# Feature maps with one ScalarE operation, an in-place min on GpSimd and the VectorE join; third layer's tokens scaled on ScalarE

## The chip, the core and the metric

The kernel runs on one core of a Trainium2 chip. A core has five engines that run their own instruction streams in order: TensorE (PE, matrix products into PSUM), VectorE (DVE), ScalarE (ACT), GpSimd (POOL) and SyncE (SP, which here issues DMAs). They wait for each other through semaphores. The metric is the device time of one execution in microseconds (us), the median of several runs.

## The reference

`x` is 2048 tokens of 1024 values (one batch). Four layers are applied, each as `x = x + f(layernorm(x))`: layer 0 and layer 2 are a linear attention with the same weights, layer 1 and layer 3 a gated feed-forward block (3584 wide) with the same weights. Of the attention, this is what matters here:

```python
q, k, v = split(x @ wqkv)                              # 32 heads of 32
phi = lambda t: where(t > 0, t + 1, exp(t)) + 1e-6     # the feature map
pq, pk = phi(q), phi(k)
kv = einsum("bhsd,bhse->bhde", pk, v)
z  = einsum("bhsd->bhd", pk)
o  = einsum(pq, kv) / (einsum(pq, z) + 1e-6)
return o @ wo
```

The feature map can be written without a branch as `max(t, 0) + min(exp(t), 1) + 1e-6`, which equals `max(t, 1e-6) + exp(-max(-t, 0) + 1e-6)` up to terms of 1e-6.

## The kernel before

Tokens lie in 16 tiles of 128 (t), four of which make a quarter (q, or `sc`). The whole `x` is resident in SBUF. An attention layer (`layer_A`, l = 0 or 2) goes through these stages:

- **Layer norm** (`ln_norm`): mean and variance on VectorE, the root on ScalarE, then the scaling of a tile of 128x1024. In layer 0 and, but for its first four tiles, in layer 2 the scaling is one VectorE `tensor_scalar` (`ln_scale`, L183); the first four tiles of layer 2 use a small VectorE operation for the shift (L214) and a ScalarE `Identity` activation (L216). A DMA then transposes the tile into `xnT`.
- **Projections** of q and k. Layer 0 makes *units* (`project`, L506): eight matmuls of 128x512 into one PSUM bank, for one tile of tokens and half the columns of q or k. Units take banks from a pool of four ("a") and, every third one, from a pool of two ("b"); the last row of units (keys of the last quarter) uses the four alone. Layer 2 makes some units too, but takes the q of quarters 0 and 1 and the k of quarters 2 and 3 by a seven-product scheme (`blocks`), described below.
- **Feature map** (`phi`, L444 to L458), once for each unit or block result, 128 in all, 16 of them in units whose quarter 3 q is made later (`q3`). ScalarE writes `relu(-ps)` to an SBUF tile `e` (L448), then `exp(-e + 1e-6)` in place (L449); VectorE joins them as `max(ps, 1e-6) + e` into the bf16 home of q or k (L452, called the *join*). The join is the last reader of the PSUM bank.
- **Key sum** (`k_sum`): for each half tile of k, GpSimd adds the joined keys into `ksum` (L527; the first of each half is a copy, L525). It waits for the join.
- **Products** `k^T x` (`m_products`), folded into `wo` later.

**The seven-product scheme** (`blocks`, L656 to L727). Each of four token groups j makes four results of 128x512 from the PSUM banks X, Y, Z and an SBUF tile V, in four steps: `one` (product 1 into X, copy Y from X, product 5, copy to V), `two` (product 2 into X, feature map of X; product 6 into Y; Z = Y + V on VectorE, L712), `three` (product 7 into Y; V = Y + V on VectorE, L716; feature map of V; product 3 into Z, feature map of Z) and `four` (product 4 into Y, feature map of Y). X and Z come from pool "a", Y from pool "b". For the k blocks, called the **K blocks** from here on, groups 0 and 1 run interleaved, then groups 2 and 3 (L933), and the copies Y from X and V of groups 1 to 3 are VectorE copies (L681). In the trace the tiles are `qx`, `qy`, `qz` and `qm` (V), for q and for k alike; the k results land in `slab`.

**What sets the order.** The program is written unit by unit with a list of delayed jobs (`later`). A scheduler then fixes the instruction order on each engine, except in stretches marked `manual_schedule`, where the engines named keep the written order. On the chip each engine runs its list strictly in order, so an instruction that waits holds back all behind it.

Of the kernel before, what the change touches and what calls it, by code (L numbers as in the profile page):

```python
# [92 lines left out]
class _Net:  # L93
    def __init__(self, tc, ctx, x_d, wqkv_d, wo_d, wg_d, wu_d, wd_d, out_d):
# [39 lines left out]
        self.inner = {}  # L134
        self.later = _Later()
        self.phi_lag = 0

        from concourse.masks import make_identity
        self.ident = self.const.tile([P, P], BF16, name="ident")
# [47 lines left out]
    def ln_norm(self, layer, t):  # L187

        nc = self.nc
        if layer % 2:  # L190
            return self.ln_norm_sums(layer, t)
        src = self.xb[t] if layer == 0 else self.x[t]
        if layer == 2 and t < self.NS:
            mv = self.acc[:, 2 * t:2 * t + 2]
        else:
            stats = self.small.tile([P, 2, nc.vector.BN_STATS_DIM], F32, tag="stats")
            for c in range(2):
                self.ln_stat(t, src, c, stats)
            if layer == 2:
                mv = self.small.tile([P, nc.vector.BN_AGGR_DIM], F32, tag="mv")  # L200
                nc.vector.bn_aggr(out=mv, in_=stats)
            else:
                mv, rstd = self.ln_rstd(stats)

        def scale(rstd=None if layer == 2 else rstd):
            if rstd is None:
                with self.tc.issue_after(self.last_exp.ins):
                    rstd = self.ln_root(mv)
                return lambda: scale(rstd)
            if layer % 2 == 0 and (layer, t // QT) != (2, 0):  # L210
                return self.ln_scale(src, mv, rstd, self.xn_home(layer, t))
            xn = self.temp([P, self.D], F16, name="xnb") if layer % 2 else self.xn_home(layer, t)
            shift = self.small.tile([P, 1], F32, tag="shift")
            nc.vector.tensor_scalar(out=shift, in0=mv[:, 0:1], scalar1=rstd[:, 0:1], scalar2=-1.0,  # L214
                                    op0=ALU.mult, op1=ALU.mult)
            nc.scalar.activation(out=xn, in_=src, func=ACT.Identity, scale=rstd[:, 0:1],  # L216
                                 bias=shift[:, 0:1])
            return xn

        return scale  # L220
# [220 lines left out]
        for j in range(QT):  # L441
            self.ln_at(first + j * step, layer, q * QT + j, lag, after)

    def phi(self, ps, out):  # L444

        nc = self.nc
        e = self.temp()
        nc.scalar.activation(out=e, in_=ps, func=ACT.Relu, scale=-1.0)  # L448
        self.last_exp = nc.scalar.activation(out=e, in_=e, func=ACT.Exp, scale=-1.0, bias=self.eps6[:, 0:1])  # L449

        def join():
            self.last_phi = nc.vector.scalar_tensor_tensor(out=out, in0=ps, scalar=1e-6, in1=e,  # L452
                                                           op0=ALU.max, op1=ALU.add)

        if self.phi_lag:
            self.later.at(self.phi_lag, join)
        else:
            join()  # L458
# [21 lines left out]
    def layer_A(self, l, last_ln):  # L480
# [392 lines left out]
        def run(*lists):  # L873

            n = max(len(u) for u in lists)
            for i in range(n):
                for u in lists:
                    if i < len(u):
                        u[i]()
                        later.tick()  # L880
# [26 lines left out]
        def quarter0():  # L907
            self.phi_lag = 3 if l == 0 else 0
            run(first)
            self.phi_lag = 0  # L910

        if l == 0:
            with self.tc.manual_schedule(engines={mybir.EngineType.DVE, mybir.EngineType.SP,
                                                  mybir.EngineType.Activation}):
# [23 lines left out]
            run(row_major(k_unit, q), row_major(q_unit, q))  # L938
        if l == 0:
            run(row_major(k_unit, self.NQ - 1))  # L940
        with self.tc.manual_schedule(engines={mybir.EngineType.DVE, mybir.EngineType.Pool}):
            q3 = row_major(q_unit, self.NQ - 1)
            out0 = column_major(out_unit, 0)
# [868 lines left out]
```

## Time and profile before

| what | value |
|---|---|
| median of 3 runs | 1438.27 us (1438.09 to 1438.8) |
| the profiled execution | 1439.99 us, of which the span from the first to the last instruction is 1437.9 us |
| PE busy | 1427.1 us (99%) |
| DVE busy | 1045.2 us (73%) |
| ACT busy | 623.3 us (43%) |
| POOL busy | 309.3 us (22%) |
| projections of layer 0 | some 6 to 106 us of the span |
| projections of layer 2 | some 732 to 823 us, the K blocks from some 797 us |

An engine is busy in a stretch while one of its instructions executes. A row of the grouped views gives line, engine, operation, tiles (out<-in), shapes, count, then busy time and mean ns of one, then the engine's idle time just before the group and what ended it. A row of one line's view gives the shortest, median and longest duration. A row of the timeline gives start and duration in us and, in brackets, the idle time of the engine before it with what ended it.

### The profile page before, as it was taken

To read this page: it belongs to the slowest core of one execution; us is meant where nothing else is said; L and a number is where in the kernel's file an instruction comes from. 1 tells how busy PE (TensorE), PEld (TensorE's weight loads), DVE (VectorE), ACT (ScalarE), POOL (GpSimd) and SP (SyncE) were. 2 spreads that over 40 slices of the span, in tenths; PEclk is the share of its full clock that TensorE was granted. 3 is DMA by queue.
4 is the path that set the end of the run, shared out by engine and by line. 5 is a ranking of instruction groups with operands and counts; after the bars stand their busy time and mean duration, and the time that the engine had idled before them with its cause. 6 is when DMAs were issued, how large, how long until landed. Compare 5 with 4: busy or idle time off the path is not lost.

```text
span 1437.9 us, 21394 instructions
## 1 busy us (share of the span) xinstructions
PE 1427.1 (99%) x7720; PEld 739.7 (51%) x7748; DVE 1045.2 (73%) x2013; ACT 623.3 (43%) x1143; POOL 309.3 (22%) x220
## 2 busy tenths in 40 slices
PE   9999999999999999999999999999999999999998
PEld 4444444444455444545654444445554565555557
DVE  7978698778685666558778886866766864766895
ACT  7872564333325244332058725733443433444301
POOL 1453860010100011110032477510111011111102
PEclk9999999999999999999999999999999999999999
DMA  9950787898559999966983218998878699975575
GB/s 286 240 162 8 172 209 202 278 335 288 200 192 294 323 367 345 291 216 199 302 277 93 70 22 234 287 274 262 268 225 294 228 304 335 274 229 174 193 260 183
DMA packets 367865, 337.74 MB, mean 235 GB/s; under 512 B 110032, under 2 KB 327760, under 8 KB 366736
## 3 DMA queue, kind: packets, MB, share of 16 engines
q1 hardware_dynamic: 359184, 313.57, 73.1%
q10 hardware_dynamic: 7136, 18.88, 3.4%
q0 software_dynamic: 1440, 3.93, 0.7%
q8 instruction: 60, 0.98, 0.3%
q14 instruction: 45, 0.37, 0.1%
HBM read 246.87 MB, written 64.82 MB: 217 GB/s over the span
## 4 chain that ended last, share of the span: by engine, by line
PE 91%; DVE 3%; DMA 2%; ACT 2%; SPq 1%; issue 1%; ACTq 0%; DVEq 0%
PE ps L506 11%; PE yu L1301 9%; PE yg L1301 9%; PE xg L1301 6%; PE xu L1301 6%; PE dy L1447 6%; PE dx L1447 5%; PE i L1154 5%; PE ps L789 4%; PE zu L1301 3%; PE zg L1301 3%; PE my L588 3%; PE dyT L1489 2%; PE mv L588 2%; PE mx L588 2%; PE dy L1489 2%
## 5 line engine op out<-in xcount | busy, mean ns | idle before, releaser
L1301 PEld LDWEIGHTS <-w 128*128 128x128 f16 (+1 forms) x2768 | 270.4, 98 | 297.2 <-issue 4.6
L506 PE MATMUL ps<-w,xnT 128*128 128x512 bf16 x768 | 169.9, 380 | 0.6 <-ACT xnT L361 0.2
L1381 POOL TENSOR_TENSOR h<-m5u,m5g 128x512 f16<-128x512 f32 x28 | 37.1, 1326 | 425.3 <-DVE m5u L1377 252.5
L506 PEld LDWEIGHTS <-xnT 128*128 128x128 bf16 x768 | 74.4, 98 | 90.3 <-issue 1.8
L1301 PE MATMUL xg<-xnT,w 128*128 128x512 f16 x448 | 115.5, 379 | 0.0
L1301 PE MATMUL xu<-xnT,w 128*128 128x512 f16 x448 | 115.0, 380 | 0.0
L1489 PEld LDWEIGHTS <-h 128*128 128x128 f16 x1008 | 98.6, 98 | 12.9
L1381 POOL TENSOR_TENSOR h<-c22u,c22g 128x512 f16<-128x512 f32 x28 | 36.0, 1285 | 289.8 <-DVE c22u L1377 247.8
L1447 PEld LDWEIGHTS <-h 128*128 128x128 f16 x616 | 60.3, 98 | 71.8 <-issue 0.3
L1301 PE MATMUL yu<-s,w 128*128 128x512 f16 x376 | 96.5, 379 | 0.5 <-DVE zu L1357 0.5
L1301 PE MATMUL yg<-s,w 128*128 128x512 f16 x376 | 96.9, 379 | 0.0
L449 ACT ACTIVATE e<-e,eps 128x512 f32<-128x512 f32 x128 | 91.0, 720 | 3.2
L736 POOL TENSOR_TENSOR kvc<-pq,kvc 128x1024 f32<-128x1024 bf16 x32 | 78.5, 2452 | 53.1 <-DVE den L741 32.8
L789 PE MATMUL ps<-T,pqT 128*128 128x512 bf16 x374 | 83.0, 380 | 0.5
L1328 DVE TENSOR_TENSOR h<-yu,r 128x512 f16<-128x512 f32 x56 | 38.6, 690 | 53.8 <-PE yu L1301 53.8
L1325 ACT ACTIVATE r<-yg 128x512 f32<-128x512 f32 x56 | 33.4, 597 | 101.3 <-PE yg L1301 101.3
L527 POOL TENSOR_TENSOR kvc<-kvc,slab 128x512 f32<-128x512 f32 x46 | 57.2, 1249 | 75.9 <-DVE slab L452 72.7
L1447 PE MATMUL dx<-w,h 128*128 128x512 bf16 x327 | 72.5, 380 | 0.5
L448 ACT ACTIVATE e<-ps 128x512 f32<-128x512 f32 x92 | 54.2, 590 | 28.4 <-PE ps L506 27.9
L1154 PEld LDWEIGHTS <-x 128*128 128x128 f16 x504 | 49.3, 98 | 33.5 <-issue 1.9
L1325 ACT ACTIVATE r<-zg 128x512 f32<-128x512 f32 x56 | 32.9, 587 | 76.7 <-PE zg L1301 76.7
L748 POOL TENSOR_TENSOR pq<-pq,den 128x1024 bf16<-128x1024 bf16 x32 | 61.1, 1909 | 6.8 <-DVE den L743 6.8
(286 smaller groups left out, 2630.6 us busy)
## 6 DMA issues: line engine op xcount, KB each, us to landing
w<-in_B_W_gate_dram SPq DMA_DIRECT2D x56, 512.0 KB, 6.4
w<-in_B_W_up_dram SPq DMA_DIRECT2D x56, 512.0 KB, 6.0
w<-ddT SPq DMA_DIRECT2D x21, 896.0 KB, 6.4
w<-td SPq DMA_DIRECT2D x18, 896.0 KB, 5.0
w<-dd SPq DMA_DIRECT2D x18, 896.0 KB, 5.9
x<-away SPq DMA_DIRECT2D x30, 512.0 KB, 7.5
away<-x SPq DMA_DIRECT2D x24, 512.0 KB, 8.1
w<-in_B_W_down_dram SPq DMA_DIRECT2D x12, 896.0 KB, 6.1
```

Of the source, the lines that this page charges most:

```text
L449: self.last_exp = nc.scalar.activation(out=e, in_=e, func=ACT.Exp, scale=-1.0, bias=self.eps6[:, 0:1])
L506: nc.tensor.matmul(by_row(ps), lhsT=self.xnT[l, l_q][:, kt, j * P:(j + 1) * P], rhs=w[:, kt, :].rearrange("p (b i d) -> p i b d", i=R, d=H ...
L588: nc.tensor.matmul(banks[j], lhsT=A(i)[:, j * P:(j + 1) * P], rhs=B(i), start=start and i == 0, stop=i == NS - 1, skip_group_check=True)
L736: nc.gpsimd.tensor_tensor(out=prod, in0=pq_of[sc, j], in1=zrow, op=ALU.mult)
L748: nc.gpsimd.tensor_tensor(out=heads(pq), in0=heads(pq), in1=den[:, :].unsqueeze(2).to_broadcast([P, D // HD, HD]), op=ALU.mult)
L789: nc.tensor.matmul(ps, lhsT=pqT[sc][:, g, j * P:(j + 1) * P], rhs=T[g // 4][:, g % 4, n2 * NW:(n2 + 1) * NW], start=(g == 0), stop=(g == G ...
L1154: nc.tensor.matmul(b[:, w, :], lhsT=B[p][:, w, k, :], rhs=A[p][:, k, :], start=start and w == 0 and k == 0, stop=k == 1, skip_group_check= ...
L1301: nc.tensor.matmul(ps, lhsT=W[w][m][:, k, :], rhs=A[m][:, k, :], start=start and k == 0, stop=k == 3, skip_group_check=True)
L1325: self.last_relu = nc.scalar.activation(out=out, in_=ps, func=ACT.Relu)
L1381: nc.gpsimd.tensor_tensor(out=h[:, 3, :], in0=V["u"], in1=V["g"], op=ALU.mult)
L1447: nc.tensor.matmul(banks[j], lhsT=A(k)[:, j * P:(j + 1) * P], rhs=w[:, i, :], start=start and k == 0, stop=k == self.U - 1, skip_group_che ...
L1489: nc.tensor.matmul(out, lhsT=A[i // 2][:, i % 2, j * P:(j + 1) * P], rhs=B[m][:, i, :], start=start and i == 0 and j == 0, stop=i == NK - ...
```

## The change

Two edits. In `phi`, under a flag that is set from the first quarter of an attention layer to the end of its q and k projections (112 of the 128 feature maps), ScalarE now does one operation, `e = exp(ps)` straight from PSUM (or from V); GpSimd does `e = min(e, 1) + 1e-6` in place; the VectorE join is `max(ps, 0) + e`. The 16 maps of `q3` stay as they were. In `ln_norm`, the `tensor_scalar` scaling remains for layer 0 only: the other twelve tiles of layer 2 now go the way of its first four (a 128x1 shift on VectorE, the scaling on ScalarE).

```diff
@@ in __init__
         self.phi_lag = 0
+        self.phi_pool = False
@@ in ln_norm
-            if layer % 2 == 0 and (layer, t // QT) != (2, 0):
+            if layer == 0:
                 return self.ln_scale(src, mv, rstd, self.xn_home(layer, t))
@@ phi
-    def phi(self, ps, out):
+    def phi(self, ps, out, low=1e-6):
         nc = self.nc
         e = self.temp()
-        nc.scalar.activation(out=e, in_=ps, func=ACT.Relu, scale=-1.0)
-        self.last_exp = nc.scalar.activation(out=e, in_=e, func=ACT.Exp, scale=-1.0, bias=self.eps6[:, 0:1])
+        if self.phi_pool:
+            low = 0.0
+            self.last_exp = nc.scalar.activation(out=e, in_=ps, func=ACT.Exp)
+            nc.gpsimd.tensor_scalar(out=e, in0=e, scalar1=1.0, scalar2=1e-6, op0=ALU.min, op1=ALU.add)
+        else:
+            nc.scalar.activation(out=e, in_=ps, func=ACT.Relu, scale=-1.0)
+            self.last_exp = nc.scalar.activation(out=e, in_=e, func=ACT.Exp, scale=-1.0,
+                                                 bias=self.eps6[:, 0:1])
         def join():
-            self.last_phi = nc.vector.scalar_tensor_tensor(out=out, in0=ps, scalar=1e-6, in1=e,
+            self.last_phi = nc.vector.scalar_tensor_tensor(out=out, in0=ps, scalar=low, in1=e,
                                                            op0=ALU.max, op1=ALU.add)
@@ in layer_A, ahead of the first quarter
+        self.phi_pool = True
         if l == 0:
...
             run(row_major(k_unit, self.NQ - 1))
+        self.phi_pool = False
         with self.tc.manual_schedule(engines={mybir.EngineType.DVE, mybir.EngineType.Pool}):
```

The scheduler also places the instructions anew. Three places matter for what follows.

GpSimd, K blocks of layer 2. `kvc` holds `ksum`; rows that end in `slab_1` add the columns 0 to 511 or 512 to 1023 of tiles 8 to 11 (results X and Z), rows that end in `slab_3` those of tiles 12 to 15 (V and Y). Before:

```order
L527 TENSOR_TENSOR kvc_6878<-kvc_6878,slab_1_7604 128x512 [waits DVE_49,Pool_49] x2
L527 TENSOR_TENSOR kvc_6878<-kvc_6878,slab_3_7636 128x512 [waits DVE_49]
L527 TENSOR_TENSOR kvc_6878<-kvc_6878,slab_1_7604 128x512 [waits DVE_49,Pool_49]
L527 TENSOR_TENSOR kvc_6878<-kvc_6878,slab_3_7636 128x512 [waits DVE_49,Pool_49]
L527 TENSOR_TENSOR kvc_6878<-kvc_6878,slab_1_7604 128x512 [waits DVE_49,Pool_49]
L527 TENSOR_TENSOR kvc_6878<-kvc_6878,slab_3_7636 128x512 [waits DVE_49]
```

After the change, from the min of X of group 0 (the last of the first row) to the sums of the first two groups:

```order
L452 TENSOR_SCALAR e<-e 128x512 [waits DVE_49,Activation_49]
L534 TENSOR_TENSOR kvc_6886<-kvc_6886,slab_1_7628 128x512 [waits DVE_49]
L452 TENSOR_SCALAR e<-e 128x512 [waits Activation_49]
L534 TENSOR_TENSOR kvc_6886<-kvc_6886,slab_1_7628 128x512 [waits DVE_49]
L452 TENSOR_SCALAR e<-e 128x512 [waits Activation_49] x2
L534 TENSOR_TENSOR kvc_6886<-kvc_6886,slab_3_7660 128x512 [waits DVE_49]
L452 TENSOR_SCALAR e<-e 128x512 [waits Activation_49]
L534 TENSOR_TENSOR kvc_6886<-kvc_6886,slab_1_7628 128x512 [waits DVE_49,Pool_49]
L452 TENSOR_SCALAR e<-e 128x512 [waits Activation_49]
L534 TENSOR_TENSOR kvc_6886<-kvc_6886,slab_3_7660 128x512 [waits DVE_49,Pool_49]
L452 TENSOR_SCALAR e<-e 128x512 [waits Activation_49] x2
```

The mins of the eight results of groups 0 and 1 now stand between the key sums on the same list, in the order X0, X1, V0 and Z0, V1, Z1, Y0 and Y1; the three rows that follow in the list (not shown) are the sums of Z1, Y0 and Y1, and only then come the mins of X2 and X3.

VectorE, K blocks, where group pair 0, 1 meets pair 2, 3. Before:

```order
L452 SCALAR_TENSOR_TENSOR slab_3_7636<-qm_7598,e 128x512 [waits DVE_49,Activation_49]
L681 COPY qy_7693<-qx_7688 128x512 [waits PE_49]
L452 SCALAR_TENSOR_TENSOR slab_1_7604<-qz_7628,e 128x512 [waits Activation_49]
L681 COPY qm_7700<-qv_7695 128x512 [waits DVE_49,PE_49]
L452 SCALAR_TENSOR_TENSOR slab_3_7636<-qy_7577,e 128x512 [waits Activation_49]
L452 SCALAR_TENSOR_TENSOR slab_3_7636<-qy_7591,e 128x512 [waits Activation_49]
L681 COPY qy_7707<-qx_7702 128x512 [waits DVE_49,PE_49]
L681 COPY qm_7714<-qv_7709 128x512 [waits PE_49]
```

After the change:

```order
L459 SCALAR_TENSOR_TENSOR slab_3_7660<-qm_7622,e 128x512 [waits DVE_49,Pool_49]
L459 SCALAR_TENSOR_TENSOR slab_1_7628<-qz_7652,e 128x512 [waits Pool_49]
L688 COPY qy_7717<-qx_7712 128x512 [waits PE_49]
L459 SCALAR_TENSOR_TENSOR slab_3_7660<-qy_7601,e 128x512 [waits Pool_49]
L459 SCALAR_TENSOR_TENSOR slab_3_7660<-qy_7615,e 128x512 [waits Pool_49]
L688 COPY qm_7724<-qv_7719 128x512 [waits DVE_49,PE_49]
L688 COPY qy_7731<-qx_7726 128x512 [waits DVE_49,PE_49]
L688 COPY qm_7738<-qv_7733 128x512 [waits PE_49]
```

The joins now wait for GpSimd instead of ScalarE, and the copies of Y2 and V2, which TensorE needs for groups 2 and 3, each stand behind more joins than before: the copy of Y2 behind the join of Z1, the copy of V2 behind the joins of Y0 and Y1.

GpSimd, layer 0, keys of the last two quarters (`slab_2` and `slab_3`). Before, the list held key sums alone there. After the change:

```order
L452 TENSOR_SCALAR e<-e 128x512 [waits Activation_49] x2
L534 TENSOR_TENSOR kvc_160<-kvc_160,slab_2_826 128x512 [waits DVE_49]
L452 TENSOR_SCALAR e<-e 128x512 [waits Activation_49] x2
L534 TENSOR_TENSOR kvc_160<-kvc_160,slab_3_1097 128x512 [waits DVE_49]
L452 TENSOR_SCALAR e<-e 128x512 [waits Activation_49]
L534 TENSOR_TENSOR kvc_160<-kvc_160,slab_3_1097 128x512 [waits DVE_49]
```

Two mins stand to one key sum while q and k units alternate, and one to one in the last row of k units.

## The prediction

> **What bounds the kernel now.** I read the busy line first, then the busy times by stretch, then the chain of waits inside the one stretch where TensorE is not full.
>
> ```profile
> PE 1427.1 (99%) x7720; PEld 739.7 (51%) x7748; DVE 1045.2 (73%) x2013; ACT 623.3 (43%) x1143; POOL 309.3 (22%) x220
> 20.00:125.00 105.00, 104.89 (x487) 47.57 (x487) 88.16 (x168) 77.72 (x141) 41.84 (x30) 1.00 0.65 185
> 732.00:835.00 103.00, 102.24 (x471) 46.09 (x472) 89.12 (x163) 80.17 (x146) 38.34 (x32) 1.00 0.37 109
> 800.00:823.00 23.00, 22.47 (x103) 10.01 (x103) 18.10 (x28) 16.87 (x29) 13.78 (x12) 1.00 0.29 92
> L506 PE MATMUL ps<-w,xnT 128*128 128x512 bf16 x391 | 84.6, 379 | 0.0
> ```
>
> The stretch rows read: length, then busy time of PE, weight load, DVE, ACT, POOL, then the clock. In the projections of layer 0 (20 to 125 us) TensorE idles 105.00 - 104.89 = 0.11 us, in those of layer 2 (732 to 835 us) 103.00 - 102.24 = 0.76 us, and 0.53 us of that lies in the K blocks. The change touches nothing that TensorE does, and the clock is 1.00 throughout, so **0.9 us is all that can be won**. What can be lost is open: every feature map holds a PSUM bank, and what is late there stops TensorE. The unit matmuls come every 84.6 / 391 = 0.216 us, so a unit of eight takes 1.73 us.
>
> The chain that ended last, in the K blocks (start, length, what):
>
> ```profile
> 804.47 0.69 DVE qm L716
> 805.19 1.11 ACT e L448 x2
> 806.30 1.22 ACT e L449 x2
> 807.52 1.00 ACT e L448 x2
> 808.52 0.62 ACT e L449
> 809.16 0.65 DVE slab L452
> 810.58 0.69 DVE qy L681
> 811.85 0.61 DVE qm L681
> 812.50 1.02 PE qv L690 x4
> ```
>
> From 804.5 to 812.5 us the chain leaves TensorE and runs through V of group 0, four ACT operations for V0 and Z0, three for V1 and Z1, the join of V1 and the copies of Y2 and V2. TensorE arrives with hardly any time to spare. In the units of layer 0 it never leaves TensorE.
>
> **The change part by part.** Prices of the operations:
>
> ```profile
> L448 ACT ACTIVATE e<-ps 128x512 f32<-128x512 f32 x92 | 54.2, 590 | 28.4 <-PE ps L506 27.9 <-DVE stats L166 0.4
> L449 ACT ACTIVATE e<-e,eps 128x512 f32<-128x512 f32 x128 | 91.0, 720 | 3.2
> L452 DVE SCALAR_TENSOR_TENSOR slab<-ps,e 128x512 bf16<-128x512 f32 x30 | 20.5, 683 | 8.5 <-ACT e L449 8.3
> L452 DVE SCALAR_TENSOR_TENSOR slab<-qm,e 128x512 bf16<-128x512 f32 x4 | 4.4, 1089 | 2.6 <-ACT e L449 2.6
> L527 POOL TENSOR_TENSOR kvc<-kvc,slab x46: 1151/1158/1532, 18.0 to 827.5; 128x512 f32<-128x512 f32 x46
> L525 POOL CAST kvc<-slab x2: 609/611/613, 14.7 to 17.5; 128x512 f32<-128x512 bf16 x2
> L183 DVE TENSOR_SCALAR slab<-x,mv,rstd 128x1024 bf16<-128x1024 f32 x8 | 8.5, 1056 | 1.2 <-ACT rstd L177 1.1
> L216 ACT ACTIVATE x<-x,shift,rstd 128x1024 bf16<-128x1024 f32 x3 | 3.7, 1232 | 0.0
> ```
>
> *ScalarE.* 112 maps lose one operation. The exp now reads PSUM, as the old relu did at 0.59 us, against 0.59 + 0.72 = 1.31 us for both: 112 x 0.72 = 81 us off an engine at 43%. The scaling of twelve layer-2 tiles adds 12 x 1.23 = 14.8 us to it and takes about 12 x 1.06 = 12.7 us from VectorE. Outside the K blocks neither engine sets TensorE's pace, so both are worth 0 by themselves, at best the 0.2 us of layer-2 idle time outside the K blocks. In the chain above the relus go: V1's exp would end some 1.9 us earlier (three relus of about 0.6).
>
> *GpSimd.* 112 in-place min-and-add operations on 128x512 f32. The trace has no such operation. The nearest rows: one input, same size, the CAST at 0.61 us; two inputs, same size, the key sum at 1.16. One input is the nearer kin, but it reads four bytes here and does two operations; I take **0.65 us**, bounds 0.61 and 1.16.
>
> The Trainium skill ("GPSIMD Engine Reference", section Performance versus the Vector engine) gives 769 ns for the best case of a loop over 512 elements. By that the K blocks below would cost about 1.2 us more; no run here shows the operation, and the CAST of 0.61 is already under that figure.
>
> *K blocks of layer 2.* GpSimd's list there has, by the order after the change, up to the min of Z1: six mins and the key sums of X0, X1, V0, Z0, that is 6 x 0.65 + 4 x 1.16 = 8.5 us of work. X0 is ready for the first min when its exp ends:
>
> ```profile
> 800.67 0.60 ACT L448 ACTIVATE e<-qx 128x512 f32<-128x512 f32 x1 [1.97 <-PE qx L690]
> 811.32 1.02 PE L690 MATMUL qx<-w,xnT 128*128 128x512 bf16 x4 [0.32 <-DVE qy L681]
> 814.30 1.02 PE L690 MATMUL qx<-w,xnT 128*128 128x512 bf16 x4
> 813.57 0.68 DVE L681 COPY qy<-qx 128x512 f32<-128x512 f32 x1
> ```
>
> so at 801.3. Without idle time GpSimd would finish at 809.8. But the sum of X0 waits for its join (about 1.0 us of idle, a VectorE addition and a join of 0.68), and the joins of V0 and V1 take two SBUF operands: the row of `qm` shows 1.09 us against 0.68, so they and GpSimd hold each other up, some 0.6 us each. That makes 809.8 + 1.0 + 1.2 = 812.0 for the min of Z1, then its join (0.68) and the copy of Y2 (0.69), which now stand in this order: 813.4. TensorE's second product of group 2 started at 811.32 behind that copy: **+2.1 us**. Then GpSimd sums V1 and does the mins of Y0 and Y1 (1.16 + 1.30, and 0.3 of waiting): 814.5, join of Y1, and the copies of V2 and Y3, which end near 816.5. TensorE took the copy of Y3 (813.57 + 0.68) at 814.30: +2.2, plus about 0.7 because its product 5 of group 3, behind the copy of V2, no longer overlaps. In the second pair the mins of X2 and X3 stand behind three key sums (3.5 us), and X2's join stands ahead of the addition for Z3, about +1.1 us more. Sum for the K blocks: 2.2 + 0.7 + 1.1 = **+4.0 us**. Ten mins lie on this path, so each 0.1 us of the min's price is worth 1 us: 3.6 at 0.61, 9 at 1.16. If the waits of 2.2 us are all hidden, it is 0.5 or less. What comes after has cover: the second key product (mx) of `m_products` starts 32 matmuls, 6.9 us, after the last K product.
>
> *Layer 0.* Here the cover is PSUM: six banks in rotation, so a join may end 5 x 1.73 = 8.6 us after its unit; 5.2 us in the last row.
>
> ```profile
> 76.60 0.60 ACT L448 ACTIVATE e<-ps 128x512 f32<-128x512 f32 x1 [0.21 <-PE ps L506]
> 81.23 0.68 DVE L452 SCALAR_TENSOR_TENSOR pq<-ps,e 128x512 bf16<-128x512 f32 x1
> 40.00:60.00 20.00, 20.00 (x95) 9.03 (x94) 20.00 (x35) 14.88 (x30) 9.52 (x8) 1.00 0.91 247
> 60.00:80.00 20.00, 20.00 (x94) 9.07 (x93) 18.66 (x35) 17.14 (x33) 8.62 (x7) 1.00 0.77 211
> L527 POOL TENSOR_TENSOR kvc<-kvc,slab 128x512 f32<-128x512 f32 x14 | 19.1, 1361 | 32.3 <-DVE slab L452 29.5 <-DVE mv L170 2.6
> L1230 DVE TENSOR_TENSOR wd<-wd x28: 631/685/1643, 43.8 to 305.3; 128x1024 f16<-128x1024 bf16 x28
> L1230 DVE TENSOR_TENSOR wd<-wd 128x1024 f16<-128x1024 bf16 x16 | 14.6, 910 | 0.1
> L183 DVE TENSOR_SCALAR x<-x,mv,rstd 128x1024 bf16<-128x1024 bf16 x8 | 4.3, 531 | 0.0
> ```
>
> The last three groups are of 40 to 80 us. VectorE is busy 38.66 of these 40 us, and the worst join ends at 81.91, 5.3 us after its unit. The weight sums of L1230 take 0.685 in the median but up to 1.64 us, and 0.91 in this stretch, where key sums take 1.36 instead of 1.16: the two hold each other up. If they exclude each other wholly, the shared time was 14 x 1.16 + 16 x 0.685 + 4.3 = 31.5 of 40 us; 23 mins of 0.65 make it 46.5, 6.5 too many. The worst join would then end 5.3 + 6.5 = 11.8 us after its unit, 3.2 beyond the cover. If collisions fall into gaps, nothing. I take **+1.0** (0 to 3.2; about 12 us more work at the dear min, then up to 6).
>
> The Trainium skill ("SBUF — State Buffer", section SBUF: two separate sides) states that GpSimd and a VectorE operation with two SBUF inputs or in a 2-port mode take a common port pair by turns, exclusively. By that rule the whole 3.2 us would fall due; were the port shared in part, 0. The 1.64 us of L1230 agrees with the rule; how much of it reaches TensorE it does not say.
>
> *Sum.* 4.0 + 1.0 + 0 = +5.0 us. The profiled execution of 1439.99 (span 1437.9, 2.1 around it) lies 1.7 over the median of 1438.27; on the profiled one it gives 1445.0, on the median **1443.3 us**, 0.35% slower.
>
> **The rivals.** *Not slower.* With the relus gone ScalarE's part of the K chain shrinks by 1.9 us, and if GpSimd's starts fall so that its idle time and the collisions vanish, 801.3 + 8.5 + 1.4 of join and copy = 811.2, just what TensorE waited for. Then only the 0.9 us of idle time and the join order act: 1437.4 to 1440.5, say 1438.2. For it: GpSimd is busy only 13.78 of 23 us there. Against: sixteen mins add 10.4, which makes 24.2 of 23. It decides at a min under about 0.5 us or a chain without waits.
>
> *The min costs as a two-input operation* (1.16 us): K blocks 9, layer 0 about 5: 1452. For it: two arithmetic operations. Against: one operand to read, and the CAST.
>
> *Layer 0 becomes the bound*: VectorE, full from 40 to 80 us, loses the shared port by turns and TensorE runs out of banks at 75 to 85 us: 3.2 us or more there, and little in layer 2, since removed L183 operations give VectorE room: 1442 to 1446, by another place than I forecast.
>
> **How the numbers follow.** Forecast (K blocks, 2 to 8 us in all) 0.53; not slower 0.27; dear min 0.13; layer 0 alone 0.07. A difference under 0.2% (2.9 us) can't be told from none. Faster by more would need 2.9 us where 0.9 is idle: 0.03, for what no row shows. The same: the other 0.24 of the first rival and 0.06 of the forecast's low end, 0.30. Slower: 0.67. The range leaves out the gain and the far end of the dear min: 1438.3 to 1452; the likeliest case's own range is 1440.3 to 1446.3.
>
> **What would show it.** Right: PE's idle time in the K blocks, waits for the copies of Y and V, grows from 0.53 us to some 4.5, with GpSimd near full from 801 to 830 us; the min's group at 0.6 to 0.8 us; less than 2 us of new PE idle time from 20 to 125. Wrong: PE still at 22.5 of 23 us in the K blocks; a min over 1 us; PE idle time in layer 0 above that of the K blocks; L1230 in the stretch to 80 us no longer than 0.91 on average.

## The result and the profile after

The changed kernel takes **1587.62 us** in the median (1585.88 to 1589.11), against 1438.28 (1438.09 to 1438.8): ratio 1.104, 95% interval 1.1018 to 1.1056. The profiled execution has a span of 1584.1 us. The forecast was 1443.3 us, range 1438.3 to 1452: the sign was right, the size off by 144 us.

In the kernel after, the lines are L451 (exp), L452 (min), L459 (join), L513 (units), L534 (key sum), L688 and L697 (copies and products of the blocks), L595 (`m_products`), L1239 (weight sums). The busy line, and the group of the min on GpSimd:

```profile
PE 1464.4 (92%) x7720; PEld 746.6 (47%) x7748; DVE 1040.0 (66%) x2013; ACT 562.8 (36%) x1043; POOL 530.9 (34%) x332
L452 POOL TENSOR_SCALAR e<-e 128x512 f32<-128x512 f32 x112 | 220.2, 1966 | 109.5 <-ACT e L451 101.3
```

One min takes 1.97 us, not 0.65. GpSimd's share of 34% again says nothing; the stretches do. The last join of layer 0's keys now ends near 185 us (106 before) and that of the K blocks near 970 us (826 before). TensorE begins layer 2 at 804 us (730 before), so 74 us of the loss, about half, fall ahead of layer 2 and the rest in it. By stretch (length, then busy time of PE, weight load, DVE, ACT, POOL, clock):

```profile
20.00:60.00 40.00, 31.78 (x133) 13.35 (x132) 24.05 (x44) 11.09 (x29) 37.18 (x24) 0.91 0.67 174
60.00:120.00 60.00, 38.61 (x153) 15.46 (x151) 31.18 (x50) 13.97 (x32) 50.44 (x30) 0.94 0.41 117
120.00:186.00 66.00, 37.97 (x137) 14.55 (x136) 20.77 (x29) 8.94 (x15) 53.92 (x33) 0.87 0.26 80
808.00:920.00 112.00, 80.67 (x320) 33.51 (x319) 55.81 (x110) 40.71 (x75) 98.74 (x57) 0.89 0.26 78
920.00:972.00 52.00, 31.87 (x120) 12.75 (x120) 19.79 (x30) 8.12 (x16) 48.68 (x31) 0.84 0.13 41
```

GpSimd is busy 82 to 94% of each, and TensorE, full before, 58 to 79%. VectorE has gone down too: it now waits. What TensorE waited for (total us, times, longest):

```profile
PE ps L513 <- DVE pq L459: 46.2, 20, 5.8
PE ps L513 <- DVE slab L459: 17.1, 12, 2.5
PE mx L595 <- DVE slab L459: 12.2, 6, 5.1
PE qx L697 <- DVE qy L688: 10.3, 2, 9.1
PE qy L697 <- DVE qz L719: 8.5, 4, 2.8
```

Joins (L459), which still hold the PSUM banks, come first, and only then the copies of Y in the K blocks (`qy`) and the additions for Z in the q blocks (`qz`). All name VectorE, yet the chain that ended last shows what stands behind the joins (start, length, what; pauses under 0.1 us left out):

```profile
119.10 1.53 POOL kvc L534
120.71 1.93 POOL e L452
122.67 0.69 DVE pq L459
123.36 0.61 DVE wd L1239
123.99 0.69 DVE wd L1239
124.68 0.69 DVE slab L459
125.44 1.52 POOL kvc L534
```

This is a ring. The key sum waits for the join of k (`slab`); the next two mins stand behind the key sum on GpSimd's list; the next join of k waits for the second of them (it runs beside the join of q and the two weight sums); the next key sum waits for that join. One turn takes 125.44 - 119.10 = 6.34 us and holds one q and one k unit, for which TensorE needs 2 x 1.73 = 3.46. TensorE is not in it. Its parts are one key sum (1.53), two mins (3.9), one join (0.69) and small gaps.

### The profile page after: what moved, and what is told of

Read it like the earlier page. It is cut to its first block, busy times and chain, and to the rows that moved or that the text cites. A ratio compares the mean times of both kernels' runs of the same rounds, so it can differ in the third digit from the quotient of the medians.

```text
span 1584.1 us, 21368 instructions
## 1 busy us (share of the span) xinstructions
PE 1464.4 (92%) x7720; PEld 746.6 (47%) x7748; DVE 1040.0 (66%) x2013; ACT 562.8 (36%) x1043; POOL 530.9 (34%) x332
## 4 chain that ended last, share of the span: by engine, by line
PE 74%; POOL 15%; DVE 6%; issue 2%; ACT 2%; DMA 1%; SPq 0%; ACTq 0%; POOLq 0%; DVEq 0%
POOL e L452 12%; PE yu L1310 8%; PE yg L1310 8%; PE dy L1456 7%; PE xg L1310 6%; PE xu L1310 6%; PE dx L1456 5%; PE i L1163 4%; PE ps L796 4%; POOL kvc L534 4%; PE zu L1310 3%; PE zg L1310 3%; PE my L595 3%; PE dyT L1498 2%; PE dy L1498 2%
## 5 line engine op out<-in xcount | busy, mean ns | idle before, releaser
L513 PE MATMUL ps<-w,xnT 128*128 128x512 bf16 x768 | 191.4, 403 | 71.5 <-DVE pq L459 46.2
L452 POOL TENSOR_SCALAR e<-e 128x512 f32<-128x512 f32 x112 | 220.2, 1966 | 109.5 <-ACT e L451 101.3
L513 PEld LDWEIGHTS <-xnT 128*128 128x128 bf16 x768 | 77.7, 102 | 179.7 <-issue 105.1
L451 ACT ACTIVATE e<-ps 128x512 f32<-128x512 f32 x76 | 43.6, 592 | 95.8 <-PE ps L513 95.8
L459 DVE SCALAR_TENSOR_TENSOR pq<-ps,e 128x512 bf16<-128x512 f32 x46 | 31.6, 687 | 68.5 <-POOL e L452 48.5
L1477 POOL DMA_DIRECT2D out_dram<-xo x30 | 19.7, 657 | 141.4 <-DVE xo L1476 141.4
L534 POOL TENSOR_TENSOR kvc<-kvc,slab 128x512 f32<-128x512 f32 x46 | 57.8, 1259 | 21.8 <-DVE slab L459 20.4
```

Source lines behind the costliest of these rows:

```text
L451: self.last_exp = nc.scalar.activation(out=e, in_=ps, func=ACT.Exp)
L452: nc.gpsimd.tensor_scalar(out=e, in0=e, scalar1=1.0, scalar2=1e-6, op0=ALU.min, op1=ALU.add)
L513: nc.tensor.matmul(by_row(ps), lhsT=self.xnT[l, l_q][:, kt, j * P:(j + 1) * P], rhs=w[:, kt, :].rearrange("p (b i d) -> p i b d", i=R, d=H ...
L534: nc.gpsimd.tensor_tensor(out=ksum[:, cols], in0=ksum[:, cols], in1=pk, op=ALU.add)
```

## The experiments

The times of the kernel before beside these runs were 1438.4 to 1438.9 us.

### Which of the two edits

The scaling of layer 2 alone on ScalarE, then the feature maps alone:

```diff
(before, in ln_norm)
-            if layer % 2 == 0 and (layer, t // QT) != (2, 0):
+            if layer == 0:
(after, in ln_norm)
-            if layer == 0:
+            if layer % 2 == 0 and (layer, t // QT) != (2, 0):
```

> Only the scaling of the layer-2 tiles moves to ScalarE; the feature maps are those of the kernel before. Theory (the price of GpSimd's min-and-add, 1.97 us on average in the changed kernel, makes the whole loss): 1437.4 to 1439.5 us, TensorE idle between 732 and 835 us not over 0.8 us. Rival (the moved scaling delays the transposed tiles or the roots on ScalarE and carries a part of the loss): over 1441 us.

> Only the feature maps change; the layer-2 scaling stays on VectorE. Theory (price of the min): 1583 to 1592 us, as the changed kernel. Rival (the moved scaling has a share in the loss): under 1580 us.

The scaling alone takes 1440.94 us, ratio 1.0016 [1.0007, 1.0025]; the maps alone 1587.56, ratio 1.1036 [1.1021, 1.1051]. So the maps alone make the whole loss, and beside them the scaling adds nothing; by itself it costs 2.3 us where I had 0, a time between the two that were forecast for it. TensorE's new waits in the run of the scaling, quoted below, include a copy that now stands on ScalarE's list behind a scaling of 1.23 us:

```profile
PE ps L506 <- DVE pq L452: 0.8, 1, 0.8
PE qx L690 <- ACT qy L683: 0.5, 1, 0.5
```

### With no min at all

```diff
-            nc.gpsimd.tensor_scalar(out=e, in0=e, scalar1=1.0, scalar2=1e-6, op0=ALU.min, op1=ALU.add)
-            low = 0.0
+            low = 1e-6
```

> The min is left out, so the map is max(q, 0) + exp(q) + 1e-6 and the join waits for ScalarE again; everything else is as in the changed kernel. Theory (GpSimd's list alone makes the loss): 1437.4 to 1440 us. Rival (the exp from PSUM, the shift of joins or the new instruction order costs by itself): over 1445 us.

> The min is left out and the layer-2 scaling stays on VectorE, so that of the change only the single exp from PSUM remains (the map is not the reference's). Without a min the changed kernel took 1442.1 us, and the moved scaling alone costs 2.3 us. Theory (the two add up): 1439 to 1440.5 us. Rival (the single exp, with the order that the scheduler makes for it, carries the difference): 1441 us or more.

1442.14 us (ratio 1.0026 [1.0015, 1.0036]), and with the scaling as before 1441.55 (1.0019 [1.001, 1.0028]). The first lies between its two forecasts; in the second the rival held. Two things follow. Of the 149 us, 145 hang on the min. And the relief of ScalarE, from 623.3 to 549.1 us of busy time in the second run, wins nothing: the single exp without any min is 2.8 us slower than before.

### What a GpSimd operation of this size costs

Six forms by turns in place of the min, each on a line of its own:

```diff
+            L455 tensor_scalar(add)               L457 tensor_scalar(mult, add)
+            L459 tensor_scalar(min)               L462 tensor_scalar(min, add), on two halves
+            L464 tensor_copy                      L466 tensor_tensor(subtract)
```

> The map's second step on GpSimd is one of six forms in turn (so the map is not the reference's): add alone; multiply and add; min alone; min and add in two halves of 256; a copy; a two-input subtract. Measured so far: min and add 1.92 us, min alone 1.49, key sum (two inputs) 1.16, CAST 0.61. Theory A (a one-input operation with a scalar costs about 1.05 us for 512 elements and 0.43 us more for each arithmetic operation, whichever it is): add 1.49, multiply and add 1.92, min 1.49, half of 256 about 1.0 to 1.05, copy 0.6 to 0.7, subtract 1.15. Theory B (min is the dear one): add at most 1.1, multiply and add at most 1.5.

Shortest, median and longest ns of each line:

```profile
L455 POOL TENSOR_SCALAR e<-e x19: 1497/1507/1562, 13.3 to 901.6; 128x512 f32<-128x512 f32 x19
L457 POOL TENSOR_SCALAR e<-e x19: 620/620/1092, 15.8 to 904.9; 128x512 f32<-128x512 f32 x19
L459 POOL TENSOR_SCALAR e<-e x19: 1485/1491/2027, 19.1 to 906.8; 128x512 f32<-128x512 f32 x19
L462 POOL TENSOR_SCALAR e<-e x38: 1066/1069/1577, 20.7 to 910.7; 128x256 f32<-128x256 f32 x38
L464 POOL COPY e<-e x18: 611/611/1069, 23.4 to 898.1; 128x512 f32<-128x512 f32 x18
L466 POOL TENSOR_TENSOR e<-e x18: 1035/1041/1489, 24.0 to 898.7; 128x512 f32<-128x512 f32 x18
```

The price goes neither by operands nor by the count of operations. Multiply and add, two operations, take 0.62 us, as a copy does; one add or one min alone 1.5; min and add 1.92. Theory A thus held for the single operations and failed for multiply and add. A second set (multiply; min, max; max, add; min, multiply; add, multiply; multiply, min) ran the same way:

> Six more forms in turn (the map is not the reference's): multiply alone; min then max; max then add; min then multiply; add then multiply; multiply then min. Theory (only multiply and add, in this order, has a short loop; any other one-input operation with scalars takes the long one, 1.49 us for one arithmetic operation and 1.92 for two): multiply alone 1.49, all others 1.92. Rival (min and max are dear, multiply and add cheap): add then multiply and multiply alone at 0.62.

```profile
L455 POOL TENSOR_SCALAR e<-e x112: 607/1922/2463, 10.4 to 913.8; 128x512 f32<-128x512 f32 x112
```

All six share a line. In the order in which they start, the 112 operations repeat with a period of six, medians 1.49, 0.61, 1.93, 1.93, 0.62 and 1.93 us: in program order, the single multiply is dear, the pairs (min, max) and (add, multiply) are cheap, and the three pairs that mix a comparison with arithmetic are the dearest. The theory had only the single multiply and the three mixed pairs right. That starts follow program order is an inference; the next runs test it for (min, max).

### The price alone: four prices for the same place

One operation (min alone), multiply and add, and min and max; in the first and the last 1e-6 goes back into the join:

```diff
-  scalar1=1.0, scalar2=1e-6, op0=ALU.min,  op1=ALU.add
+  scalar1=1.0, scalar2=None, op0=ALU.min                      (e3)
+  scalar1=1.0, scalar2=1e-6, op0=ALU.mult, op1=ALU.add        (e9)
+  scalar1=1.0, scalar2=0.0,  op0=ALU.min,  op1=ALU.max        (e13)
```

> GpSimd does the min alone, one arithmetic operation instead of two; the 1e-6 stays in the join. Theory A (the price goes by the number of arithmetic operations): about 1.0 to 1.1 us for one, so two mins and a key sum of 1.26 take 3.4 us against 3.45 us of TensorE work for a pair of units, and the time is 1438 to 1465 us. Theory B (the price belongs to this form of instruction, whatever it computes): 1.9 us and 1580 to 1595 us.

> GpSimd multiplies by one and adds 1e-6 (0.62 us in the run of prices) where it did min and add (1.92 us); the min is left out, so the map is not the reference's; everything else is as in the changed kernel. The prediction assumed 0.65 us, so this is its case: by its sum 1443 us (K blocks +3.7, layer 0 +1.0), by the runs of the moved scaling and of the left-out min (+2.5 and +3.7 without any GpSimd step) rather 1444 to 1449 us. Rival (the hop over GpSimd costs by itself, in waits and collisions, whatever its price): over 1460 us.

> The change with GpSimd doing min(e, 1) and then max with 0 in one operation (the exp is never negative, so the max changes nothing), and 1e-6 back in the join; the same map as the reference's. In the run with six forms in turn one form of two operations that I take for this pair lasted 0.61 us, as multiply and add did; min and add 1.92. Theory of two causes (the price of the form, and a ring between GpSimd and VectorE): the min's group at about 0.65 us and the same time as with multiply and add, 1475 us (1470 to 1480). Rival, that the price was the only thing wrong in the prediction: 1443 us. Third reading, that the fast slot was another form: the group at 1.5 to 1.9 us and 1530 to 1590 us.

| form | mean us of one | median us | ratio, 95% |
|---|---|---|---|
| min, add (the change) | 1.97 | 1587.6 | 1.1037 [1.1018, 1.1056] |
| min | 1.55 | 1531.7 | 1.0648 [1.0634, 1.0663] |
| multiply, add | 0.67 | 1475.3 | 1.0252 [1.0238, 1.0266] |
| min, max | 0.67 | 1469.5 | 1.0215 [1.02, 1.023] |
| none | - | 1442.1 | 1.0026 [1.0015, 1.0036] |

The row of min and max:

```profile
L452 POOL TENSOR_SCALAR e<-e x112: 603/612/1146, 10.8 to 854.4; 128x512 f32<-128x512 f32 x112
```

So the same map can be had at a third of the price, and 118 of the 149 us are the price. But at 0.67, close to the 0.65 that I had assumed, the change still costs 31 us where I had predicted 5. The rival "the price was the only thing wrong" (1443) falls, and with multiply and add the rival that the way over GpSimd costs by itself held. The single min came out between both its forecasts, as its price did.

### What goes round with the mins

Without the key sums, and with the mins for q alone (k maps and scaling as before):

```diff
(e6, in k_sum)
-                nc.gpsimd.tensor_tensor(out=ksum[:, cols], in0=ksum[:, cols], in1=pk, op=ALU.add)
(e12, in phi; only the calls for q pass q=True)
-        if self.phi_pool:
+        if self.phi_pool and q:
```

> The changed kernel without the 56 key sums on GpSimd (only the first copy of each half stays, so the denominator is not the reference's). Theory (what GpSimd has to do in all sets the pace: 112 mins of 1.97 us and 56 sums of 1.28 us against 188 us of TensorE work): the 72 us of the sums go in full, and up to 36 us of GpSimd's waiting with them: 1480 to 1516 us. Rival (each min is late by itself, through the bank it holds, and the sums matter little): over 1560 us.

> Only the maps of q go over GpSimd (48 of 96 in that stretch and the 8 of the first quarter per layer 0, 56 at most), those of k as before, scaling as before. Theory (a sum over GpSimd's list, against TensorE's time for the same stretch, decides): a pair of one q and one k unit needs 1.95 + 1.26 = 3.2 us of GpSimd against 3.45 us of TensorE, the K blocks have no min at all, so most of the loss goes: 1440 to 1460 us. Rival (each map over GpSimd costs its share): half of the 149 us, 1512 us.

1505.63 us (ratio 1.0465 [1.0447, 1.0482]) and 1489.16 (1.0348 [1.0332, 1.0364]). Without key sums GpSimd runs mins back to back, as its timeline shows (start, length, count at the end), here eight in 15.92 us, 1.99 each:

```profile
99.56 15.92 POOL L452 TENSOR_SCALAR e<-e 128x512 f32<-128x512 f32 x8
```

Nothing of a ring is left; GpSimd, busy 98.87 of the 105 us from 20 to 125, sets the time by its bare rate, 2 x 1.99 = 3.98 us a pair against 3.46. In the changed kernel's trace these were 60 sums, not 56 as the expectation has it. With the mins for q alone (48 in the trace) the time lies between the two forecasts: GpSimd is far from full, yet TensorE is slow, by the windows from 40 to 100 us:

```profile
40.00:100.00 60.00, 45.12 (x194) 19.21 (x193) 38.26 (x69) 28.02 (x59) 40.12 (x26) 0.97 0.59 153
```

GpSimd is busy 40 of 60 us and TensorE 45. Its list in that run:

```profile
113.28 1.16 POOL L534 TENSOR_TENSOR kvc<-kvc,slab 128x512 f32<-128x512 f32 x1 [1.47 <-DVE slab L459]
114.52 1.92 POOL L452 TENSOR_SCALAR e<-e 128x512 f32<-128x512 f32 x1
117.91 1.15 POOL L534 TENSOR_TENSOR kvc<-kvc,slab 128x512 f32<-128x512 f32 x1 [1.47 <-DVE slab L459]
```

Sum, min, 1.47 us for two joins in a row (of q, which waits for the min, then of k), sum: 4.63 us a turn. The turn needs 3.46 us of TensorE, 75% of it, and 75% is what TensorE is busy in the window. So the ring accounts for an engine that is a third idle and still the cause.

### The key sums moved

Issued five steps after its map instead of one, with GpSimd's list kept as written in the projections, each key sum stands behind the mins of later maps and waits for a join that is old:

```diff
-            later.at(1 + (10 if self.phi_lag else 0), lambda: k_sum(...))
+            later.at(5 + (10 if self.phi_lag else 0), lambda: k_sum(...))
-                    later.at(1, lambda: k_sum(t, cols))
+                    later.at(5, lambda: k_sum(t, cols))
+            with self.tc.manual_schedule(engines={mybir.EngineType.Pool}): (around the projections)
```

> The change with every key sum written five steps later and GpSimd's list kept as written through the projections, so that a key sum stands behind the mins of later maps and waits for a join that is old. Min and add stay. Ring theory: the period of a pair of maps falls from sum + two mins + join with their waits, about 5.9 us, to GpSimd's bare work 2 x 1.97 + 1.2 = 5.1 us; 28 pairs of layer 0 and about as many maps of layer 2, so 25 to 45 us less: 1542 to 1562 us. Rival, GpSimd is simply full and the order of its list costs nothing: 1587 us, within 5.

> Both: min and max in one operation, and the key sums five steps later. Ring theory: GpSimd's work per pair, 2 x 0.62 + 1.2 = 2.4 us, now hides in TensorE's 3.45, and the time comes near that without any min, 1442.1: 1442 to 1452 us. Rival, that the two engines hold each other up operation by operation (key sums up to 1.5 us, joins late for it) and the list order matters little: 1465 to 1475 us. If the min's group is at 1.5 us or more, the run says nothing of this.

With min and add 1565.23 us (ratio 1.0883 [1.0867, 1.0899]), 22.4 less, so the order of the list does cost, a little less than the 25 to 45 forecast; from 40 to 100 us GpSimd is then busy 56.92 of 60 us: full, there is nothing left to reorder. With min and max 1460.32 (1.0158 [1.0141, 1.0175]), 9.1 less than in the change's order, but far from the 1442 to 1452 expected; both theories missed. Of the 18 us that are left over the run without any min, two causes show in the trace. One is the move itself. The last key sums now end late, and ScalarE's list waits for them (L539), with the copy (L580) that TensorE needs behind it, 4.5 us. The timeline at that place:

```profile
842.64 5.09 POOL L534 TENSOR_TENSOR kvc<-kvc,slab 128x512 f32<-128x512 f32 x4
...
845.35 1.37 DVE L566 TENSOR_TENSOR x<-x,slab 128x512 f16<-128x512 bf16 x1
846.65 1.37 DVE L566 TENSOR_TENSOR x<-x 128x512 f16<-128x512 bf16 x1
847.76 1.06 ACT L539 ACTIVATE e<-kvc 128x1024 bf16<-128x1024 f32 x1 [6.22 <-POOL kvc L534]
...
848.27 0.41 DVE L566 TENSOR_TENSOR x<-x 128x512 f16<-128x512 bf16 x1
848.61 0.41 DVE L566 TENSOR_TENSOR x<-x,xn 128x512 f16<-128x512 f16 x1
...
849.36 0.81 PE L595 MATMUL mx<-slab,slab 128*128 128x512 bf16 x3 [4.53 <-ACT my L580]
```

The other cause shows on the same lines: a VectorE addition of two SBUF tiles takes 1.37 us while key sums run, and 0.41 for the same shape once they have ended. VectorE's weight sums in layer 0 are operations of this kind.

### The weight sums left out

```diff
(in sums_d)
-            self.nc.vector.tensor_tensor(out=out, in0=a, in1=b, op=ALU.subtract)
+            if not self.phi_pool:
+                self.nc.vector.tensor_tensor(out=out, in0=a, in1=b, op=ALU.subtract)
```

> Min and max in one operation, with VectorE's sixteen weight sums (wd from wd, L1243 in the run with late key sums, L1230 in the kernel before) left out of the projections of layer 0; so that part of a later layer's weights is not computed. In the run with late key sums and the cheap form these sums last 1.15 us against 0.68 at their shortest between 40 and 100 us, and the mins beside them are stretched too. Theory that VectorE's two-operand sums and GpSimd hold each other up: of the 6.5 us of TensorE idle time from 40 to 100 us, 4 to 6 go, and what the order of the list costs in the last row of k units (100 to 112 us, no weight sums there) stays: 1463 to 1466 us against 1469.5. Rival, the ring of key sums alone: nothing changes there, 1468 to 1471.

> The run with min and max and late key sums, without the same sixteen weight sums. Holding up: TensorE is full from 40 to 100 us (53.6 of 60 us before), 5 to 7 us less than 1460.3: 1453 to 1456 us; what remains over 1442 is then the end of the K blocks, where the late sums hold up ScalarE's list (4.5 us in one wait), the like of it after layer 0 (1.9) and layer 2. Rival, the mins' later joins alone make TensorE wait in layer 0: 1459 to 1462 us.

1460.05 us (ratio 1.0145 [1.013, 1.0161]), 9.4 less than 1469.5, and 1452.53 (1.0095 [1.0078, 1.0112]), 7.8 less than 1460.3, both somewhat more than forecast. The edit leaves out twenty sums, not sixteen: the trace has 28 with them and 8 without, and four of the twenty ran after 100 us, among the last k units. The stretch from 80 to 100 us, min and max with the change's list, with and without these sums (one row from each of the two kernels' windows):

```profile
80.00:100.00 20.00, 17.52 (x81) 7.69 (x80) 12.43 (x19) 5.97 (x10) 13.17 (x16) 1.00 0.58 173
```

```profile
80.00:100.00 20.00, 20.00 (x95) 9.04 (x94) 7.83 (x13) 6.59 (x12) 14.84 (x19) 1.00 0.49 152
```

VectorE was not full in the first (12.4 of 20). That does not clear it, for in the ring its list counts and not its share. The chain of the run with min and max and the weight sums, in the same stretch:

```profile
80.88 1.53 POOL kvc L534
82.41 0.59 POOL e L452
83.03 0.69 DVE pq L459
83.72 0.61 DVE wd L1239
84.35 0.69 DVE wd L1239
85.04 0.61 DVE slab L459
85.72 1.53 POOL kvc L534
```

Two weight sums stand on VectorE's list between the join of q and the join of k. This turn takes 85.72 - 80.88 = 4.84 us; one without weight sums beside it, from 94.52 to 97.66, takes 3.14, less than TensorE's 3.46. Of the 1.7 us between them, 1.3 are the two sums themselves, in series, and 0.4 the key sum, which takes 1.53 us beside a weight sum and 1.16 without. From 40 to 100 us the weight sums hold 10.0% of the chain, 6.0 us. So most of what they cost here is plain time on VectorE's list inside the ring, and the mutual hold-up that the theory named is the smaller part. Between 40 and 100 us the mean min goes from 0.68 to 0.62 us and the key sum from 1.31 to 1.20 without these sums. With late key sums it is otherwise: there the chain from 81.2 to 92.2 us runs over VectorE alone, through joins and seven weight sums of 0.98 to 1.54 us, 9.1 in all, where the shortest takes 0.68. A run that keeps VectorE's time and takes away only the second SBUF operand was not made.

From 100 to 120 us, mostly keys alone, TensorE stays at 15.4 of 20 us with four weight sums there, and at 16.1 with none; there the ring needs no help. GpSimd's list with min and max:

```profile
121.36 1.16 POOL L534 TENSOR_TENSOR kvc<-kvc,slab 128x512 f32<-128x512 f32 x1 [0.81 <-DVE slab L459]
122.48 0.61 POOL L452 TENSOR_SCALAR e<-e 128x512 f32<-128x512 f32 x1
123.91 1.16 POOL L534 TENSOR_TENSOR kvc<-kvc,slab 128x512 f32<-128x512 f32 x1 [0.81 <-DVE slab L459]
```

A turn of 123.91 - 121.36 = 2.55 us holds one unit of 1.73.

### The scaling, once more; the min on VectorE; the clock

```diff
(e16: e15 with)
-            if layer == 0:
+            if layer % 2 == 0 and (layer, t // QT) != (2, 0):
(e7)
-            nc.gpsimd.tensor_scalar(out=e, in0=e, scalar1=1.0, scalar2=1e-6, op0=ALU.min, op1=ALU.add)
+            nc.vector.tensor_scalar(out=e, in0=e, scalar1=1.0, scalar2=None, op0=ALU.min)
+            low = 1e-6
(e8: after, ahead of each layer-0 unit from the second on)
+                for i in range(4):
+                    nc.tensor.matmul(warm, lhsT=self.ones, rhs=w[:, i, :], start=True, stop=True)
```

> As the run with both, with the third layer's scaling back on VectorE as before the change. Without any min the scaling moved cost 0.6 us (1442.1 against 1441.6), alone 2.3. Ring theory: 0.5 to 2.5 us less than the run with both. Rival, VectorE is now the tight one and the moved scaling helps it: 1 to 3 us more than the run with both.

> The min goes to VectorE, in place, ahead of the join (one operation, the 1e-6 stays in the join); the rest as in the changed kernel. Theory (GpSimd's price alone is the matter; on VectorE a 128x512 f32 min is well under 0.69 us, though VectorE is full from 40 to 80 us): 1440 to 1455 us. Rival (a third instruction in the chain between matmul and join is what stops TensorE, whichever engine does it): over 1500 us.

> The changed kernel with four matmuls of 128x512 without use (0.86 us) ahead of each unit of layer 0 but the first, to fill TensorE's idle time there. The granted clock of the changed kernel is 0.87 to 0.94 from 20 to 186 us. Theory (the lower clock is a result: GpSimd sets the pace and TensorE has time to spare): clock 0.98 or more in that stretch, time 1583 to 1595 us. Rival (the lower clock carries a part of the loss, TensorE's busy time having grown from 1427 to 1464 us): under 1578 us.

*Scaling.* 1463.35 us (1463.01 to 1465.56), against 1460.32 (1459.12 to 1462.9) with the scaling moved: the move wins 3.0 us here, where alone it lost 2.3. The rival held. That the sign hangs on which of the two engines is late is argued, not shown.

*VectorE.* 1466.18 us (ratio 1.0192 [1.0177, 1.0207]), between the two forecasts. One min takes 0.58 us there and needs no turn on GpSimd's list, but VectorE is then full, and TensorE at 94 of 105 us, from 20 to 125:

```profile
20.00:125.00 105.00, 93.81 (x426) 41.52 (x426) 102.63 (x183) 35.79 (x80) 38.80 (x32) 1.00 0.72 192
```

*Clock.* In the changed kernel the granted clock is 0.84 to 0.94 in the slow stretches. With useless matmuls in TensorE's gaps of layer 0 it is higher there (1.00, 0.97 and 0.96 from 20 to 60, 120 and 186 us, against 0.91, 0.94 and 0.87), and the time is longer all the same: 1596.95 us (1.1099 [1.1083, 1.1116]). The row from 60 to 120 us, useless matmuls included in PE:

```profile
60.00:120.00 60.00, 49.74 (x216) 21.64 (x218) 26.38 (x42) 13.87 (x32) 48.24 (x29) 0.97 0.44 119
```

The low clock goes with the idle time; raising it did not shorten the projections, and the rival (under 1578 us) falls. The time is 2 us over the theory's range, and the useless matmuls take time on TensorE's own list, so this run alone does not bound what the clock carries. The chain of the changed kernel does: from 20 to 180 us mins hold 53.9% of it, key sums 21.6%, and TensorE nothing; from 808 to 972 us TensorE holds some 5%.

None of these versions beats the kernel before. Where the time went, from single runs, each of the last three steps by one part alone:

| kernel | us | step |
|---|---|---|
| before | 1438.4 | |
| one exp, scaling moved, no min (e4) | 1442.1 | +3.7 |
| mins at 0.65 us, key sums late, no weight sums (e18) | 1452.5 | +10.4 |
| with the weight sums (e15) | 1460.3 | +7.8 |
| key sums where the change has them (e13) | 1469.5 | +9.1 |
| min and add, 1.97 us (the change) | 1587.6 | +118.1 |

The steps hang on their order (the late sums are worth 22.4 us at the dear form, 7.5 without the weight sums). The step of 10.4 changes three parts at once (mins, late key sums, weight sums left out). In its trace TensorE's waits are 5.1 us behind ScalarE's copy in `m_products`, 3.5 for joins of q and 3.0 for the copies and Z of the blocks; which part brings each was not tested.

## Why the prediction was wrong

**The price of the min: the step that failed most.** "One input is the nearer kin, but it reads four bytes here and does two operations; I take 0.65 us, bounds 0.61 and 1.16." Measured 1.97. Both bounds came from operations of another kind, and nothing in the rows said that the key sum was an upper bound; I treated the next dearer row as one. The Trainium skill ("GPSIMD Engine Reference", section Performance versus the Vector engine) gives 769 ns as the best case of a loop over 512 elements. The trace differs on both sides: the copy and the pairs of 0.62 us lie under that figure, and min and add, at 1.92, is 2.5 times it.

**The rule from price to time.** "Each 0.1 us of the min's price is worth 1 us" was counted over the ten mins of the K blocks. From 0.67 to 1.97 us the runs show 118.1 / 13 = 9.1 us for each 0.1, as the mins of both layers count, not ten, once GpSimd's turn is longer than TensorE's. The slope is not even: 62.2 us from 0.67 to 1.55 (7.1 for each 0.1), 55.9 from 1.55 to 1.97 (13.3, more than the 11.2 of 112 mins; no run tells where the excess comes from). The prediction never compared rates: two mins and a key sum make 2 x 1.16 + 1.36 = 3.7 us even at its own dear price, more than the 3.46 of a pair of units. The rival with 1.16 us and 1452 was too cheap by its own rows.

**Layer 0, "+1.0 (0 to 3.2)".** I set a fixed excess of work against the PSUM cover of 8.6 us. That is right for a single burst, and wrong for a ring, which loses in each turn until the cover is gone. With min and max at 0.67 us, near my assumption, TensorE's waits for joins are 6.4 us up to 100 us and 6.7 from 100 to 140 (3.8 of them in `m_products`, behind the last joins). The order that I quoted for GpSimd (two mins, a key sum that waits for VectorE, two mins) showed the ring; I read it as a sum of work, not as a chain of waits.

**The hold-up between VectorE and GpSimd** was seen and priced as optional ("if collisions fall into gaps, nothing"). It does not fall into gaps: 9.4 us go with the weight sums. The place, "L1230 in the stretch to 80 us", was the right one to name, but the reason only in part: the larger share is the sums' own time between two joins of the ring (1.3 of 1.7 us a turn), the smaller the stretched key sum. How far the two engines exclude each other shows beside the late key sums: there the additions of L566 start 1.29 us apart, where one key sum alone (1.16) and one addition alone (they start 0.34 us apart) make 1.50. So they take turns for most of the time, though not the whole. The Trainium skill ("SBUF — State Buffer", section SBUF: two separate sides) states that the turns are exclusive. The trace agrees for the larger part, and by the 0.2 us between 1.29 and 1.50 it does not.

**The K blocks, "+4.0".** At the price that I had assumed this term was nearly right. With min and max TensorE's waits in the K blocks are 3.1 us, for the copy of Y2, as the working had it, and 0.4 for that of V2: 3.5 in all, some 3.0 more than the 0.5 idle before. The parts fit less well than the sum: the 1.1 us of the second pair did not come. The working also has a slip: 812.0 + 1.16 + 1.30 + 0.3 is 814.8 and not 814.5, which makes the term 4.3. At 1.97 us the waits for copies and V there are 10.3, 2.5 and 1.1 us. But "what comes after has cover" was wrong: in `m_products` of layer 2 TensorE waits 2.3 us more behind ScalarE with min and max, and in the change 5.5 us for joins and 4.2 behind ScalarE.

**ScalarE and the scaling, "0".** The relief indeed wins nothing. The terms are +2.8 for the single exp and +2.3 for the scaling alone, 3.7 together. Every list is put in another order by either edit, which is a likely reason but not a tested one; beside late key sums the scaling moved is worth -3.0.

**The rivals.** "Not slower" had a chance of 0.27 on a GpSimd that was "busy only 13.78 of 23 us". "Layer 0 becomes the bound" was given 0.07, and it happened for half of the loss, 74 us, chiefly by GpSimd's list and not by the shared port alone; its "little in layer 2" was as wrong as my own forecast, for the other half lies there. The range ended at 1452 because no case let the new operation cost more than any row shown. An operation without a row should have widened it by far.

## What to carry to other kernels

Before work is moved to an idle engine, compare its rate with the stage's: all that it will do per turn, at a price measured for this very form, against what the bounding engine needs per turn. Then follow the list for rings: an in-order engine that both feeds another engine's operation and waits for its result behind the next item on its list adds these times up, and with them all that stands in between on the other engine's list, however idle both look. For a price without a row, no neighbouring row is an upper bound; one run with several forms by turns gives them all.

## What was not expected of the hardware

On GpSimd, in place on 128x512 f32: copy, multiply and add, add and multiply, min and max 0.61 to 0.62 us; a single add, min or multiply 1.49 to 1.51; min and add, max and add, min and multiply, multiply and min 1.92 to 1.93. A dummy second operation of the same sort thus makes a min 2.4 times as fast (1.49 to 0.61). Half the tile takes 1.07 of 1.92 us. VectorE does the single min in 0.58. For multiply alone, add and multiply, and the mixed pairs other than min and add, the price rests on the order of starts in one run. Why the single operations are slow, no run here tells.
